# Batch 0's head: x loaded ahead of the weights, group 0's tile from scores of tokens and shifted tokens, groups 1 to 3 from the regular stage B, other idle products

## The chip, the core and the metric

The kernel runs on one NeuronCore of a Trainium2 chip. TensorE (PE) multiplies and transposes into PSUM, VectorE (DVE), ScalarE (ACT) and GpSimd (POOL) do the elementwise work, SyncE (SP) issues nearly all DMA transfers, in order, on one queue. The metric is device microseconds of one execution, the median of the runs.

## The reference

Two layers follow each other on x of shape (4, 12608, 128). The first is attention through 32 learned inducing points; the second is a channel mix with a token shift. `w_k`, `w_v` and `w_r` come as float64, the rest as float32.

```python
h = mab(I, x)            # 32 inducing rows attend to 12608 tokens of a batch
a = mab(x, h)            # every token attends to the 32 rows of h
a_prev = shift(a, 1)     # the token before, zeros ahead of the first
xk = mu_k * a + (1 - mu_k) * a_prev
xr = mu_r * a + (1 - mu_r) * a_prev
v = relu(xk @ w_k) ** 2 @ w_v        # 128 -> 1024 -> 128
out = sigmoid(xr @ w_r) * v
# mab(q, kv): a = softmax(q @ kv.T / sqrt(128)), with 1e-9 added to the sum; a @ kv
```

Since `a = A @ h` with A of 32 columns, the kernel never forms `a`. It folds h into the weights (`W`, from `h * mu_k` and `h * (1 - mu_k)` times `w_k`; `Wg` likewise with `w_r`) and multiplies the attention weights A of a token and of the token before it by them.

## The kernel before

The four batches are worked on one after the other. A batch has 6 full blocks of 2048 tokens and a tail of 320 tokens. A full block is 4 groups of 512 tokens.

**Stage A** of a batch computes h: transpose x (`xt`), scores against the inducing rows, a running maximum, exponentials, and the sums `acc` and `sum`. For batch 0 it runs ahead of everything else, as the **head** (`stage_a_head`, called from `head`, L908 to L943): the blocks come in the order tail, 0 to 5, and for each block the order is maximum, exponentials, the product of the block before, transposes of the block after next, transposes of the exponentials, scores of the next block. For batches 1 to 3 it is spread over the units of the batch before (`stage_a`).

**Loads in the head.** SP's queue takes x in half blocks of 512 KB (L192, L211) and between them the weights (L95) in pieces of 512 KB, raw 64-bit words: two of `w_k`, two of `w_v`, one of 128 KB of `w_r`. Each weight piece is turned into float32 by six steps on VectorE, ScalarE and GpSimd (`exponent`, `mantissa`, `clamp`, `sign`, `low`, `power`, L103 to L133), and `w_v` is then split into a high and a low part (`wvh`, `wvl`, L160). These steps wait in the list `work`; `place(n)` emits the next n of them, and the table `PARTS` says how many at which point of which block.

**Combine** (`combine`) turns `acc` and `sum` into `hT` and `h4`; `wpart` then makes `W` and `Wg`. `spin` (L889) issues products whose results nobody reads, between the last transposes and the last block's product.

**Stage B** makes the tile R of a group: the scores of its tokens against h, a softmax over 32 rows, and the weights A split into a high and a low part, two slices of 512 columns. R has 128 rows: rows 0 to 31 the tokens, 32 to 63 the shifted tokens, 64 to 127 the same again. The regular `stage_b` handles a block of four groups: a 32 x 32 transpose on VectorE, maximum, subtraction, exponential, sum, reciprocal, product, transpose back, high and low part (`hl`); then `spread(i)` fills R of group i with three DMA transfers (one first column from the group before, rows 0 to 31, rows 32 to 63), and `double` copies rows 0 to 63 to 64 to 127 with one. All of them go through SP's queue.

Block 0 of batch 0 has its own code, `stage_b_head` (L684), called twice, for groups 0 and 1 and for groups 2 and 3. It turns the weights with TensorE and copies 32 rows at a time: for group 0 eight copies fill all 128 rows (L744 and L745, ScalarE and VectorE in turn), for groups 1 to 3 one copy each for the tokens and for the shifted tokens (L738, L739), the first column by DMA from the group before, and `double`.

**The unit loop** (L999) is the bulk of the time. A unit is a quarter of the hidden columns of one group: 4 units a group, 25 groups and 100 units a batch, 400 in all. Unit n does: six products of `up` (L782, for two units at every even n) into PSUM, `square` (relu on VectorE, L792; its square twice on ScalarE, L797 and L798; the low part on GpSimd, L800; at the units in `high_vector` the square that is rounded is VectorE's, L794), and six products of `down` (L811) of the unit four before. At units that are 1 modulo 4 `zgate` computes the sigmoid (L770, L772).

Everything else is hung on the units by `at(n, f)`: f is emitted at the end of unit n. Block j + 1's stage B starts at unit t + 12j + 1 of its batch and stage A of the next batch's block j at t + 12j, where t is

```python
t = b * UB + (1 if b == 0 else 0)     # L978, UB = 100 units
```

Stage B's exponential comes 3 units after its start, stage A's exponential 15 after its own. Both use another ScalarE table than the sigmoid; a change of table is an instruction of its own, ACT_TABLE_LOAD. There are 5 buffers for R. Each engine executes its instructions in the order in which they are emitted; the order is written out by hand.

## Time and profile before

| | |
|---|---|
| time, median of 3 runs | 1158.64 us (1156.19 to 1158.97) |
| profiled execution | 1160.58 us |
| its span | 1158.8 us |
| PE, DVE, ACT, POOL busy | 94%, 79%, 84%, 82% |
| head, to stage B's first transpose (L703) | 51.5 us |
| unit 0 begins (first L792) | 63.2 us |
| unit 4, unit 8 begin | 83.7, 103.5 us |
| batch 1's unit 0 begins | 368.6 us |
| last unit begins | 1148.2 us |

In the profile's rows stand the start in us, the duration in us, the engine, the line, the operation and `out<-in` with the shapes; what stands in brackets is the idle time of the engine ahead of it and what ended it. PEld is TensorE's loading of weights, SPq the issuing of transfers by SP. A row of a `windows` view has the window, its length, busy time and count for each engine, and at its end the granted TensorE clock (1.00 is full), the DMA engines' share and GB/s. The rows themselves stand in the prediction.

### The profile page before, as it was taken

To read this page: it belongs to the slowest core of one execution; us is meant where nothing else is said; L and a number is where in the kernel's file an instruction comes from. 1 tells how busy PE (TensorE), PEld (TensorE's weight loads), DVE (VectorE), ACT (ScalarE), POOL (GpSimd) and SP (SyncE) were. 2 spreads that over 40 slices of the span, in tenths; PEclk is the share of its full clock that TensorE was granted. 3 is DMA by queue.
4 is the path that set the end of the run, shared out by engine and by line. 5 is a ranking of instruction groups with operands and counts; after the bars stand their busy time and mean duration, and the time that the engine had idled before them with its cause. 6 is when DMAs were issued, how large, how long until landed. Compare 5 with 4: busy or idle time off the path is not lost.

```text
span 1158.8 us, 19210 instructions
## 1 busy us (share of the span) xinstructions
PE 1089.2 (94%) x6548; PEld 740.6 (64%) x6548; DVE 919.0 (79%) x1293; ACT 976.2 (84%) x1112; POOL 945.2 (82%) x413
## 2 busy tenths in 40 slices
PE   6768889889999989999999989999999999999997
PEld 4435556556667656666667656666666666677775
DVE  5666778788777979999777979999877878888665
ACT  5446879889999868989889878889898989999995
POOL 1135778768998878899988878899988999999996
PEclk9869999989999989999999989999999999999999
DMA  9212565655515566666534565676423345444422
GB/s 276 62 39 75 115 137 124 150 136 106 123 27 101 120 140 133 151 152 146 120 56 82 113 144 126 144 165 142 101 49 60 75 91 110 82 79 86 83 39 33
DMA packets 267601, 124.38 MB, mean 107 GB/s; under 512 B 225552, under 2 KB 246704, under 8 KB 265200
## 3 DMA queue, kind: packets, MB, share of 16 engines
q1 hardware_dynamic: 267168, 123.14, 49.7%
q8 instruction: 52, 0.85, 0.3%
q14 instruction: 45, 0.37, 0.1%
q10 hardware_dynamic: 336, 0.02, 0.0%
HBM read 28.07 MB, written 25.82 MB: 47 GB/s over the span
## 4 chain that ended last, share of the span: by engine, by line
PE 74%; DVE 9%; ACT 4%; DMA 4%; SPq 3%; POOL 3%; issue 2%; DVEq 0%; ACTq 0%; POOLq 0%
PE ps_v L811 41%; PE ps_a L782 23%; DVE k_t L792 4%; PE ps_v L770 3%; POOL kl L800 3%; PE pb_b L603 2%; DMA R<-R 2%; PE pb_a L361 1%; PE pb_a L430 1%; SPq L834 1%; ACT k_t L798 1%; DVE kh L794 1%; DMA xb<-in_x_dram 1%; SPq L95 1%; DMA kl<-in_x_dram 1%
## 5 line engine op out<-in xcount | busy, mean ns | idle before, releaser
L800 POOL TENSOR_TENSOR kl<-k_t,kh 128x1024 fp32r<-128x1024 f32 (+2 forms) x400 | 936.3, 2370 | 174.0 <-ACT k_t L798 136.2
L792 DVE TENSOR_SCALAR k_t<-ps_a 128x1024 f32<-128x1024 f32 (+1 forms) x400 | 477.9, 1198 | 115.7 <-PE ps_a L782 85.4
L798 ACT ACTIVATE k_t<-k_t 128x1024 f32<-128x1024 f32 (+1 forms) x400 | 418.1, 1047 | 65.2 <-DVE kh L794 30.0
L797 ACT ACTIVATE kh<-k_t 128x1024 fp32r<-128x1024 f32 (+1 forms) x352 | 365.0, 1037 | 69.7 <-DVE k_t L792 69.1
L782 PE MATMUL ps_a<-R,W 64*128 64x512 f32 (+1 forms) x2400 | 344.7, 414 | 37.6 <-DVE k_t L792 13.2
L782 PEld LDWEIGHTS ps_a<-R,W 64*128 64x128 f32 x2400 | 212.0, 187 | 167.9 <-issue 51.5
L811 PE MATMUL ps_v<-kh,wvh 128*128 128x512 f32 (+1 forms) x800 | 273.9, 424 | 1.0 <-ACT rT L772 0.9
L811 PE MATMUL ps_v<-kl,wvh 128*128 128x512 f32 (+1 forms) x800 | 249.3, 393 | 2.5 <-POOL kl L800 1.2
L811 PE MATMUL ps_v<-kh,wvl 128*128 128x512 f32 (+1 forms) x800 | 248.7, 392 | 0.0
L811 PEld LDWEIGHTS ps_v<-kh,wvh 128*128 128x128 f32 x800 | 133.3, 190 | 98.9 <-issue 42.5
L811 PEld LDWEIGHTS ps_v<-kl,wvh 128*128 128x128 f32 x800 | 150.8, 190 | 37.1 <-POOL kl L800 4.0
L811 PEld LDWEIGHTS ps_v<-kh,wvl 128*128 128x128 f32 x800 | 151.0, 190 | 33.7
L816 DVE TENSOR_TENSOR oT<-ps_v,rT 128x512 f32<-128x512 f32 (+1 forms) x100 | 67.1, 671 | 17.1 <-PE ps_v L811 16.3
L827 DVE STREAM_TRANSPOSE ot<-oT 128x512 f32<-128x512 f32 x96 | 67.1, 699 | 0.0
L770 PE MATMUL ps_v<-R,Wg 128*128 128x512 f32 (+1 forms) x198 | 61.2, 390 | 0.0
L794 DVE SCALAR_TENSOR_TENSOR kh<-ps_a,k_t 128x1024 fp32r<-128x1024 f32 x48 | 58.8, 1225 | 2.4
L772 ACT ACTIVATE rT<-ps_v 128x512 f32<-128x512 f32 (+1 forms) x99 | 57.3, 579 | 0.4
L333 DVE STREAM_TRANSPOSE xs<-xb 128x512 f32<-128x512 f32 x72 | 49.9, 694 | 7.0 <-DMA xb<-in_x_dram 6.6
L772 ACT ACT_TABLE_LOAD x35 | 44.9, 1283 | 0.6
L770 PEld LDWEIGHTS ps_v<-R,Wg 128*128 128x128 f32 x198 | 37.3, 189 | 9.1 <-DVE k_t L792 0.8
L603 PE MATMUL pb_b<-xt,hT 128*32 128x512 f32 x184 | 25.9, 637 | 3.6 <-DVE aT L703 3.6
L364 DVE TENSOR_REDUCE mx<-pb_a 128x1 f32<-128x512 f32 x18 | 12.5, 692 | 16.7 <-PE pb_a L361 16.7
(201 smaller groups left out, 543.8 us busy)
## 6 DMA issues: line engine op xcount, KB each, us to landing
R<-R SPq DMA_DIRECT2D x95, 256.0 KB, 3.1
out_dram<-ot SPq DMA_DIRECT2D x184, 128.0 KB, 3.3
xb<-in_x_dram SPq DMA_DIRECT2D x18, 1024.0 KB, 5.9
xt<-xs SPq DMA_DIRECT2D x288, 64.0 KB, 2.0
R<-hl SPq DMA_DIRECT2D x92, 128.0 KB, 2.3
R<-hl SPq DMA_DIRECT2D x92, 127.8 KB, 2.4
kh<-in_x_dram SPq DMA_DIRECT2D x4, 512.0 KB, 8.0
kl<-in_x_dram SPq DMA_DIRECT2D x4, 512.0 KB, 7.5
```

The costliest lines, as they stand in the source:

```text
L333: nc.vector.transpose(out=xs.rearrange("p (s q) -> p s q", q=M), in_=S.xb[j][:, :, M * c:M * (c + 1)])
L770: nc.tensor.matmul(out=ps[:, :w], lhsT=S.Wg, rhs=R[:, s, :w], start=(s == 0), stop=(s == 1))
L772: nc.scalar.activation(out=self.rT, in_=ps[:, :w], func=AF.Sigmoid)
L782: nc.tensor.matmul(out=ps[:, r, :w], lhsT=S.W[a][rows, u * P:(u + 1) * P], rhs=R[rows, k, :w], start=(n == 0), stop=(n == 2))
L792: nc.vector.tensor_scalar(out=k, in0=ps, scalar1=0.0, scalar2=None, op0=ALU.max)
L794: nc.vector.scalar_tensor_tensor(out=kh, in0=ps, scalar=0.0, in1=k, op0=ALU.max, op1=ALU.mult)
L797: nc.scalar.activation(out=kh, in_=k, func=AF.Square)
L798: nc.scalar.activation(out=k, in_=k, func=AF.Square)
L800: return lambda eng, a, z: eng.tensor_tensor(out=kl[:, :, a:z], in0=k[:, :, a:z], in1=kh.bitcast(F32)[:, :, a:z], op=ALU.subtract)
L811: nc.tensor.matmul(out=self.v, lhsT=wt[:, fc, :], rhs=kk[:, c, :], start=(fc == 0 and n == 0), stop=(fc == FC - 1 and n == 2))
L816: nc.vector.tensor_tensor(out=self.oT, in0=self.v, in1=self.rT, op=ALU.mult)
L827: nc.vector.transpose(out=ot[:, o:o + w], in_=self.oT)
```

## The change

The edits are these.

- **Loads.** All x of batch 0 is queued ahead of the five weight pieces, and `w_r` ahead of `w_v`. The conversion steps move to later blocks (`PARTS`): none before block 3, the conversions of `w_v` after the last block's maximum, the split of `w_v` after stage B's first steps.
- **Last block of the head.** The sum and `weights` come ahead of the transposes of the exponentials, and `weights` is cut in two (`weights`, `weights_sum`).
- **Idle products.** `spin` issues six transposes of 128 columns where there were fourteen products of 512.
- **Group 0.** `stage_b_first` takes the scores of group 0's tokens and of the same tokens shifted by one. The shifted ones are in `S.x0`, a copy that GpSimd makes early in the head in one of R's buffers. Weights of tokens and shifted tokens are laid out so that four transposes give all 128 rows of R for the high part and four for the low one; two copies fill R.
- **Groups 1 to 3** come from the regular `stage_b(0, 0)`, whose steps are called by hand: the scores to the subtraction among the steps of `stage_b_first`, the exponential in unit 0, the rest at the end of unit 0. Then `spread` and `double` run through SP's queue.
- **Unit numbers.** In batch 0 t is 4 where it was 1, so that the stages on the blocks come three units later (block 1's stage B at unit 2, one unit later). In later batches the combine's steps come one unit and block 0's stage B three units sooner.

Group 0 needs no transfer for R before or after; groups 1 to 3 needed two each and now need four. SP's queue from the load of batch 1's first block on, before (`R<-R` with 32x2x1 is the first column, `R<-R` with 64x1024 `double`, `xt<-xs` stage A):

```order
L206 DMA xb<-in_x_dram 128x2048
L336 DMA xt<-xs 32x512 x4
L570 DMA R<-R 32x2x1
L336 DMA xt<-xs 32x512 x4
L577 DMA R<-R 64x1024
L336 DMA xt<-xs 32x512 x8
L570 DMA R<-R 32x2x1
L577 DMA R<-R 64x1024
```

and with the change:

```order
L206 DMA xb<-in_x_dram 128x2048
L580 DMA R<-hl 32x2x1
L593 DMA R<-hl 32x1024
L593 DMA R<-hl 32x2x511
L587 DMA R<-R 64x1024
```

These four of group 1 are followed by the same four of group 2 and three of group 3, then by the first four `xt<-xs` and group 3's `double`.

ScalarE at a block's two exponentials in batch 0 (`e1t` is stage A's, `s` stage B's, `rT` the sigmoid), before:

```order
L397 ACT_TABLE_LOAD
L397 ACTIVATE alpha<-mkr,nb 128x1
L398 ACTIVATE e1t,ss<-pb_a,nb 128x512
L798 ACTIVATE k_t<-k_t 128x1024
L772 ACT_TABLE_LOAD
L772 ACTIVATE rT<-ps_v 128x512
L620 ACT_TABLE_LOAD
L620 ACTIVATE s_1652<-s_1652 128x512
```

and with the change:

```order
L401 ACT_TABLE_LOAD
L401 ACTIVATE alpha<-mkr,nb 128x1
L402 ACTIVATE e1t,ss<-pb_a,nb 128x512
L806 ACTIVATE k_t<-k_t 128x1024
L630 ACTIVATE s_1687<-s_1687 128x512
L805 ACTIVATE kh<-k_t 128x1024
L806 ACTIVATE k_t<-k_t 128x1024
L780 ACT_TABLE_LOAD
L780 ACTIVATE rT<-ps_v 128x512
```

The sigmoid has moved behind both exponentials, so that one table load between them is gone and the sigmoid's own one follows them. ScalarE has 26 table loads up to the 25th sigmoid before and 18 with the change.

VectorE from the copy of the last block's exponentials (`e`) to `hT`, before:

```order
L274 COPY e_654<-pb_a 128x512
L279 SCALAR_TENSOR_TENSOR sum<-sum,alpha,ss 128x1
L500 TENSOR_TENSOR ws<-sum,wt 128x1
L504 TENSOR_SCALAR rd<-pb_b 128x1
L505 RECIPROCAL rd<-rd 128x1
L508 TENSOR_SCALAR mk<-stack,wt,rd 128x32
L297 SCALAR_TENSOR_TENSOR acc<-acc,alpha,pb_a 128x128
L518 COPY hT<-pb_b 128x32
```

and with the change:

```order
L278 COPY e_643<-pb_a 128x512
L127 SCALAR_TENSOR_TENSOR s_593<-s_593,aT 128x512
L105 TENSOR_SCALAR s_647<-k_t 128x512
L514 TENSOR_SCALAR rd<-pb_b 128x1
L515 RECIPROCAL rd<-rd 128x1
L518 TENSOR_SCALAR mk<-stack,wt,rd 128x32
L115 TENSOR_SCALAR xs<-k_t 128x512
L109 TENSOR_SCALAR s_647<-s_647 128x512
L301 SCALAR_TENSOR_TENSOR acc<-acc,alpha,pb_a 128x128
L120 TENSOR_SCALAR aT<-k_t 128x512
L528 COPY hT<-pb_b 128x32
```

Five conversion steps of `w_v` have come in between. The last two of the second piece (L123, L127) stand behind `h4`, ahead of stage B's first transpose (L714); the first piece's other five stand ahead of these rows, behind the last block's maximum.

The diff, cut to its core:

```diff
+                if j == 0 and h + i == 0:
+                    S.x0 = r_pool.tile([P, 2, G], F32, name="R")[:, 0, :]
+                    nc.gpsimd.memset(S.x0[:, 0:1], 0.0)
+                    nc.gpsimd.tensor_copy(out=S.x0[:, 1:], in_=dst[:, :G - 1])
...
     def weights():
         ws = S.sum
         if ahead:
-            wt = sm.tile([P, 1], F32, name="wt")
+            wt = L["wt"] = sm.tile([P, 1], F32, name="wt")
             nc.scalar.activation(out=wt, in_=S.mrun, func=AF.Exp, bias=L["nm"], scale=scale)
             ws = sm.tile([P, 1], F32, name="ws")
             nc.vector.tensor_tensor(out=ws, in0=S.sum, in1=wt, op=ALU.mult)
+        L["ws"] = ws
...
         return prod, high, low
     if ahead:
-        return maxes, weights, hfin, wpart
-    at(t + 9, weights)
-    at(t + 10, hfin)
+        return maxes, weights, weights_sum, hfin, wpart
+    at(t + 8, weights)
+    at(t + 9, hfin)
     for gate in range(2):
         prod, high, low = wpart(gate, lambda: pb_tile("a"))
-        at(t + 11 + 2 * gate, prod)
-        at(t + 11 + 2 * gate, high)
-        at(t + 12 + 2 * gate, low)
+        at(t + 10 + 2 * gate, prod)
+        at(t + 10 + 2 * gate, high)
+        at(t + 11 + 2 * gate, low)
...
+    if at is None:
+        return scores, trans, maxi, sub, expo, total, recip, mult, back, high, low, spread
...
+def stage_b_first():
     S = batches[0]
+    n = 2 * Q
     L = {}
     def scores():
+        ps = L["ps"] = pb_tile("a")
+        pv4 = ps[:, :n * M].rearrange("(i m) (c w p) -> i m w c p", m=M, w=2, p=M)
+        for w, src in enumerate((S.xt[0, 0], S.x0)):
+            xv = src.rearrange("c (k i p) -> c i k p", i=Q, p=M)
             for i in range(Q):
+                nc.tensor.matmul(out=pv4[i, :, w], lhsT=S.hT, rhs=xv[:, i], start=True, stop=True)
     def diff():
+        s2 = L["s2"] = st.tile([P, Q, P], F32, name="e1").rearrange("p k (i m) -> p (k i) m", m=M)[:, :n, :]
         nc.vector.transpose(out=s2.rearrange("p k m -> p (k m)"), in_=L["ps"][:, :n * M])
         mx = sm.tile([P, Q * Q], F32, name="mx2")[:, :n]
         nc.vector.tensor_reduce(out=mx, in_=s2, op=ALU.max, axis=AX.X)
...
         nc.vector.tensor_scalar(out=sm2, in0=sm2, scalar1=EPS, scalar2=None, op0=ALU.add)
         nc.vector.reciprocal(out=sm2, in_=sm2)
         nc.vector.tensor_tensor(out=s2, in0=s2, in1=sm2.unsqueeze(2).broadcast_to([P, n, M]), op=ALU.mult)
+        nc.vector.memset(s2[0:1, 1, :], 0.0)
+    def src():
+        return L["s2"].rearrange("p (c w) m -> p c (w m)", w=2).unsqueeze(2).broadcast_to([P, Q, 2, 2 * M])
+    def half(s):
+        return L["a"][:, s, :].rearrange("p (c r k) -> p c r k", c=Q, r=2)
     def high():
+        L["a"] = st.tile([P, 2, G], F32R, name="hl", bufs=2)
+        nc.scalar.copy(out=half(0), in_=src())
     def low():
+        nc.vector.tensor_tensor(out=half(1), in0=src(), in1=half(0).bitcast(F32), op=ALU.subtract)
+    def turn(s):
+        if s == 0:
+            L["pt"] = pa.tile([P, 2, G], F32, name="ps_a")
+            S.R[0] = r_pool.tile([P, 2, G], F32R, name="R")
+        for c in range(Q):
+            cs = slice(c * P, (c + 1) * P)
+            nc.tensor.transpose(out=L["pt"][:, s, cs], identity=ident, in_=L["a"].bitcast(F32)[:, s, cs])
+    def put(s):
+        if s == 0:
+            nc.scalar.copy(out=S.R[0][:, 0, :], in_=L["pt"][:, 0, :])
+        else:
+            nc.vector.tensor_copy(out=S.R[0][:, 1, :], in_=L["pt"][:, 1, :])
+    return scores, diff, expo, norm, high, low, turn, put
 NG = (NBLK - 1) * Q + 1
-    def put(k, whole):
-        g = gs[k]
-        ps = pa.tile([P, 2, G], F32, name="ps_a")
-        for s in range(2):
-            for c in range(Q):
-                nc.tensor.transpose(out=ps[:M, s, c * P:(c + 1) * P], identity=ident,
-                                    in_=L["a"].bitcast(F32)[:, k * Q + c, s, :])
-        new_r(S, g)
-        R = S.R[g]
-        if not whole:
-            nc.scalar.copy(out=R[:M], in_=ps[:M])
-            nc.vector.tensor_copy(out=R[M:HP, :, 1:], in_=ps[:M, :, :G - 1])
-            return
-        nc.vector.memset(R.bitcast(F32)[3 * M:, :, 0:1], 0.0)
-        for s in range(2):
-            for r in range(2):
-                nc.scalar.copy(out=R[HP * r:HP * r + M, s], in_=ps[:M, s])
-                nc.vector.tensor_copy(out=R[HP * r + M:HP * (r + 1), s, 1:], in_=ps[:M, s, :G - 1])
-    return scores, diff, expo, norm, high, low, put
...
+wloads += [load_wr]
-wloads += [load_wr]
-    if wloads:
-        wloads.pop(0)()
-maxes, weights, hfin, wpart = combine(0)
+maxes, weights, weights_sum, hfin, wpart = combine(0)
...
-    half = P // 2
-    rhs = wvh.rearrange("p c d -> p (c d)")[:, :G]
-    for i in range(3):
-        nc.tensor.matmul(out=ps[:, i % 2, :], lhsT=wvh[:, i, :], rhs=rhs, start=True, stop=True)
-        for r in range(2):
-            rows = slice(half * r, half * (r + 1))
-            nc.tensor.matmul(out=ps[:, r, :], lhsT=wvh[rows, (i + r) % FC, :], rhs=rhs[rows],
-                             start=True, stop=True)
-    for i in range(3):
-        nc.tensor.matmul(out=ps[:, i % 2, :], lhsT=wvh[:, i, :], rhs=rhs, start=True, stop=True)
-PARTS_FIRST = 6
-PARTS = ((0, 0, 0), (3, 3, 0), (3, 3, 0), (3, 3, 0), (3, 3, 1), (1, 0, 0), (0, 0, 0))
+        nc.tensor.transpose(out=ps[:, 0, :P], in_=ident, identity=ident)
+PARTS = ((0, 0, 0), (0, 0, 0), (0, 0, 0), (0, 3, 0), (3, 3, 0), (3, 3, 1), (3, 4, 2))
...
         if k + 2 < NBLK:
             ab[k + 2].tr()
         place(PARTS[k][1])
+        if k == last:
+            ab[k].sums()
+            weights()
         ab[k].etrans()
         ab[k].ecopy()
-        ab[k].sums()
         if k < last:
+            ab[k].sums()
             ab[k + 1].scores()
         place(PARTS[k][2])
-    spin(4)
-    weights()
+    weights_sum()
+    place(2)
+    spin(6)
     ab[last].hmm()
     ab[last].acc()
     load_x(1, 0)
+    place(1)
     hfin()
-    assert not work
+    place(2)
 events = {}
...
-    sc0, df0, ex0, nm0, hi0, lo0, put0 = stage_b_head([0, 1])
-    sc1, df1, ex1, nm1, hi1, lo1, put1 = stage_b_head([2, 3])
+    scores, diff, expo, norm, high, low, turn, put = stage_b_first()
+    (b_scores, b_trans, b_maxi, b_sub, b_expo, b_total, b_recip, b_mult, b_back, b_high, b_low,
+     b_spread) = stage_b(0, 0, None, 0)
-    run([sc0, df0, wk[0], ex0, wk[1], nm0, wk[2], hi0, lo0, lambda: put0(0, True)])
-    at(0, lambda: put0(1, False))
-    for n, f in ((0, sc1), (1, lambda: double(batches[0], 1)), (1, df1), (1, ex1), (2, nm1), (2, hi1),
-                 (2, wg[0]), (2, wg[1]), (3, wg[2]), (3, lo1)):
+    run([scores, b_scores, diff, wk[0], expo, b_trans, norm, wk[1], high, wk[2], lambda: turn(0),
+         lambda: put(0), low, lambda: turn(1), b_maxi, lambda: put(1), b_sub])
+    soon(0, b_expo)
+    for n, f in ((0, b_total), (0, b_recip), (0, b_mult), (0, b_back), (0, b_high), (0, b_low),
+                 (0, wg[0]), (1, wg[1]), (1, wg[2]), (3, lambda: units[0][0].zgate())):
-    for k in range(2):
-        at(4 + 2 * k, lambda k=k: put1(k, False))
-        at(5 + 2 * k, lambda k=k: double(batches[0], 2 + k))
-    at(4, lambda: units[0][0].zgate(first=True))
+    for i in range(1, Q):
+        at(i - 1, lambda i=i: b_spread(i))
+        at(i, lambda i=i: double(batches[0], i))
+    place(len(work))
-    t = b * UB + (1 if b == 0 else 0)
+    t = b * UB + (4 if b == 0 else 0)
-        stage_b(b, j + 1, at, s + 1 if b or j else 1)
+        stage_b(b, j + 1, at, s + 1 if b or j else 2)
-        stage_b(b + 1, 0, at, s + 13)
+        stage_b(b + 1, 0, at, s + 10)
```

More of the change, by code (lines that the diff above doesn't have):

```diff
@@ L500, in weights, with weights_sum @@
                 nc.vector.tensor_tensor(out=ws, in0=S.sum, in1=wt, op=ALU.mult)
+            L["ws"] = ws
+            if not ahead:
+                weights_sum()
+        def weights_sum():
+            ws, wt = L["ws"], L.get("wt")
             ps = pb_tile(None if ahead else "b")
@@ L514, in hfin @@
         def hfin():
-            ps = pb_tile(None if ahead else "b")
+            ps = pb_tile("b")
             nc.tensor.matmul(out=ps[:, :M], lhsT=S.acc, rhs=L["sw"], start=True, stop=True)
@@ L717, in norm @@
             nc.vector.tensor_tensor(out=s2, in0=s2, in1=sm2.unsqueeze(2).broadcast_to([P, n, M]), op=ALU.mult)
+            nc.vector.memset(s2[0:1, 1, :], 0.0)
[3 more added lines that the diff above has]
+            return L["a"][:, s, :].rearrange("p (c r k) -> p c r k", c=Q, r=2)
         def high():
-            a = L["a"] = st.tile([P, 2, G], F32R, name="hl", bufs=2) \
-                .rearrange("p s t -> p (s t)")[:, :2 * n * M].rearrange("p (k s m) -> p k s m", s=2, m=M)
@@ L759, in __init__, with zgate @@
             self.v = None
-        def zgate(self, first=False):
+        def zgate(self):
             S, w = self.S, self.w
             R = S.R[self.g]
-            if first:
-                ps = pb_tile("a")
-            else:
-                ps = self.v = pv.tile([P, G], F32, name="ps_v")[:, :w]
+            ps = self.v = pv.tile([P, G], F32, name="ps_v")[:, :w]
             for s in range(2):
@@ L913, in head @@
             ab[k].tr()
-        place(PARTS_FIRST)
         ab[0].scores()
```

17 lines of the change are left out of this document (3 added, 14 removed).

## The prediction, written before the changed kernel was timed

> **What bounds the kernel now.** I read the page first, then the rate of the unit loop (one unit is one `k_t` row: 256 of the 1024 hidden columns of one 512-token group), then the stretches where it is slow, and last the head.
>
> ```profile
> span 1158.8 us, 19210 instructions
> PE 74%; DVE 9%; ACT 4%; DMA 4%; SPq 3%; POOL 3%; issue 2%; DVEq 0%; ACTq 0%; POOLq 0%
> ```
>
> Over the whole span the end is set by TensorE, which the change leaves alone nearly everywhere. The 26% of the chain that is not PE is where it can act. To place it I count units per stretch, VectorE's `k_t` instruction (L792) in chosen windows:
>
> ```profile
> 63.20:83.60 20.40, 4.89 (x4) 0.75 0.23 52
> 83.60:103.50 19.90, 4.89 (x4) 0.80 0.22 47
> 103.50:307.00 203.50, 81.66 (x68) 0.97 0.57 127
> 368.50:378.50 10.00, 4.83 (x4) 1.00 0.67 135
> 399.00:414.40 15.40, 4.83 (x4) 0.93 0.66 135
> 378.50:566.00 187.50, 82.40 (x68) 0.98 0.64 144
> 646.50:833.30 186.80, 82.39 (x68) 0.98 0.61 136
> ```
>
> Columns: window, length, busy (count), granted clock, DMA share, GB/s. Units 0 to 7 take 40.3 us; four units at the same place of batch 1 take 10.0. Units 8 to 75 take 203.5 us in batch 0, and the 68 units 96 later take 187.5 in batch 1 and 186.8 in batch 2. So batch 0 loses some 20 us in its first eight units and 16 more in the next 68, beside the 63 us ahead of unit 0.
>
> **The 16 us: what batch 0 does differently.** ScalarE's rows around the two exponentials of a block, first in batch 0, then in batch 1:
>
> ```profile
> 173.18 1.28 ACT L772 ACT_TABLE_LOAD   x1
> 174.48 0.60 ACT L772 ACTIVATE rT<-ps_v 128x512 f32<-128x512 f32 x1
> 175.09 1.28 ACT L620 ACT_TABLE_LOAD   x1
> ...
> 453.16 0.61 ACT L620 ACTIVATE s<-s 128x512 f32<-128x512 f32 x1
> ```
>
> In batch 0 a sigmoid falls between the exponential of stage A (L398) and that of stage B (L620), so each table is loaded once more. In batch 1 the two follow each other. Batch 0's blocks start at unit 1 + 12j, those of later batches at a multiple of 4, and the sigmoid comes at every unit that is 1 modulo 4. The change starts batch 0's blocks at 4 + 12j: a multiple of 4, and ScalarE's instructions stand in batch 0 as in batch 1 (the second order fence ahead).
>
> ```profile
> 103.50:307.00 203.50, 171.55 (x187) 0.97 0.57 127
> 378.50:566.00 187.50, 161.69 (x179) 0.98 0.64 144
> ```
>
> ScalarE's windows: 187 instructions and 171.6 us against 179 and 161.7. The 8 instructions are table loads, 8 x 1.28 = 10.2 us; the rest of the 16 is what waits behind them. I take the whole 16.0 (203.5 less 187.5), since work and order are then those of batch 1. One thing stays worse: block 1's first tile (unit 16) is spread at unit 12 and doubled at 14, in batch 1 at the 11th and 13th after its start, and there the four units ahead of it take 15.4 us where others take 10. One unit later is 2.6 us (187.5 / 68) at most, nothing at least, if the shorter queue ahead of it makes it up. I take 1.4. **Term: -14.6.**
>
> **The head.**
>
> ```profile
> 8.81 3.74 PE L229 MATMUL ps_a<-ident,kh 128*128 128x128 f32 x16 [4.56 <-DMA kh<-in_x_dram]
> 15.60 1.27 POOL L133 TENSOR_TENSOR wk_sb<-e1t,s 128x512 f32<-128x512 f32 x1 [14.30 <-DVE s L127]
> 25.68 1.06 PE L229 MATMUL ps_a<-ident,kl 128*128 128x128 f32 x8 [0.66 <-DMA kl<-in_x_dram]
> 29.40 0.43 DVE L105 TENSOR_SCALAR s<-k_t 128x512 int32<-128x512 int32 x1
> 31.07 0.69 DVE L123 SCALAR_TENSOR_TENSOR e1t<-k_t,e1t 128x512 f32<-128x512 uint32 x1
> 34.65 0.23 DVE L105 TENSOR_SCALAR s<-oT 128x128 int32<-128x128 int32 x1
> 38.47 0.15 DVE L250 TENSOR_SCALAR nb<-mx 128x1 f32<-128x1 f32 x1
> 42.48 0.15 DVE L250 TENSOR_SCALAR nb<-mx 128x1 f32<-128x1 f32 x1
> 44.76 0.69 DVE L274 COPY e<-pb_a 128x512 f32<-128x512 f32 x1 [0.81 <-PE pb_a L269]
> 46.48 0.97 PE L902 MATMUL ps_a<-wvh 128*128 128x512 f32 x3
> 47.50 1.08 PE L286 MATMUL pb_a<-xb,e 128*32 128x128 f32 x32
> 51.46 0.45 DVE L703 STREAM_TRANSPOSE s<-pb_b 128x256 f32<-128x256 f32 x1 [1.15 <-PE pb_b L697]
> ```
>
> Two half blocks' worth of 512 KB have landed at 8.81, twelve at 25.68: 1.69 us each. Ahead of 25.68 those twelve are four blocks and four weight pieces; now they are all of batch 0's x, and the first weight lands at 27.4, the next at 29.1, w_r at 29.5, w_v at 31.2 and 32.9. So blocks no longer wait for data, but the first conversion (L105) stands on VectorE behind block 3's maximum and waits there until 27.4; behind it in the queue is the copy of block 3's exponentials. Its three operations and that copy end at 29.3, block 4's maximum at 30.6. A block with a full conversion takes 5.2 us (L105 at 29.40, then 34.65), one without 4.0 (L250 at 38.47, then 42.48). With 5.0 and 4.5 for the two that are left the last block's maximum is done at 40.1, for 42.48 before.
>
> From there to stage B's first transpose it was 9.0 us (42.48 to 51.46). The idle products go: they end at 47.45, and the copy of exponentials that the block product at 47.50 needs is done at 45.45, so -2.0. But both w_v conversions now stand there on VectorE, four operations of 0.43 (L105) and two of 0.69 us (L123) each, 6.2 us, 6.7 with the end of w_r's, of which I put 3.1 in gaps where it waited: 9.0 - 2.0 + 3.6 = 10.6, and the transpose at 50.7. The bounds: all of the 6.7 on the path 53.8, all in gaps 47.1; the middle, because half of the rows stand behind a wait for ScalarE. The copy for shifted tokens is one GpSimd instruction of 128 x 511; a product of that size took 1.27 us there (L133), and the engine had been idle for 14.3 us ahead of it: nothing, and 1.3 if a conversion had to wait for it.
>
> **The first tile.**
>
> ```profile
> 54.27 0.42 DVE L717 TENSOR_TENSOR s<-s,sm 128x256 f32<-128x256 f32 x1
> 55.18 1.89 PE L733 MATMUL ps_a<-ident,hl 128*32 128x128 f32 x8 [2.14 <-ACT hl L722]
> 57.11 0.57 ACT L744 CAST R<-ps_a 32x512 fp32r<-32x512 f32 x1 [1.98 <-PE ps_a L733]
> 63.24 1.22 DVE L792 TENSOR_SCALAR k_t<-ps_a 128x1024 f32<-128x1024 f32 x1 [0.88 <-PE ps_a L782]
> ```
>
> From the transpose (51.46) to unit 0 it was 11.8 us, 5.3 of them the eight copies of 32 rows that ScalarE and VectorE make in turn (57.11 to 62.4). Now the tile is turned as 128 rows. To the division 3.2 as before, regular stage B's transpose in a gap 0.5, the high half 0.6 behind the weights' cast 0.4, low 0.7, four transposes 0.95, the second copy 0.7, stage B's subtraction 0.7, gaps 0.55: 8.3, and unit 0 at 59.0. **Term: -4.2** (-8 to -1 with the head's bounds).
>
> **Units 0 to 8.**
>
> ```profile
> 67.57 1.21 DVE L739 CAST R<-ps_a 32x1022 fp32r<-32x1022 f32 x1 [2.48 <-ACT R L738]
> 82.31 1.65 PE ps_a L782 x6
> 83.96 2.86 PE ps_v L811 x6
> 112.26 1.21 SPq L583 DMA_DIRECT2D R<-hl  x2
> R<-R SPq DMA_DIRECT2D x95, 256.0 KB, 3.1
> R<-hl SPq DMA_DIRECT2D x92, 127.8 KB, 2.4
> ```
>
> Groups 1 to 3 lose three times a copy on ScalarE and one of 1.21 us on VectorE (L739), 24 transposes of the kind that took 1.89 for 8, and the second small softmax. In their place each group has four transfers where it had two, in SP's queue ahead of nearly all x transposes (the first order fence ahead). Group 1: after unit 0's `k_t` (1.2) VectorE runs sum, reciprocal, product, transpose back and low half with ScalarE's high half between, 0.7 + 0.2 + 0.3 + 0.7 + 0.7 + 0.6 + 0.7 and 0.1 of gaps, to 64.2. Three issues of 0.6, landing 2.4, doubling 3.1: 71.5. Its first six products 1.65 at half clock (a row of the chain of waits, as the next): unit 4 at 73.2, for 83.66. SP waits at each doubling for the transfers ahead, so group 2 is there 4.7 us later, before unit 8 needs it. Units 4 to 7 take 10.0 as in batch 1, and 3.0 for what half a clock does to some and the start's own table loads: unit 8 at 86.2, for 103.5. Bounds: the 3.0 could be 0 or 7 and the transfers 2 us either way. **Term, beside the head's -4.2: -13.1.**
>
> From batch 1 on the combine comes one unit and the next batch's block 0 three units earlier. The four units at a batch's start take 10.0 us, so there is no stall to win: 0. If TensorE now has to wait for VectorE's `hT` (one unit lies between, where there were three), it is a microsecond at each of three boundaries, inside the bounds below.
>
> **Sum:** -4.2 - 13.1 - 14.6 = -31.9. The profiled span of 1158.8 becomes 1126.9, its execution's 1160.58 becomes 1128.7; the median of the runs shown, 1158.64, lies 1.9 below that execution, so I forecast **1127 us** as the median.
>
> **The clock.** The granted clock, in windows of all engines:
>
> ```profile
> 44.00:50.00 6.00, 4.89 (x54) 3.53 (x54) 2.45 (x11) 0.03 (x1) 0.00 (x0) 1.00 0.38 156
> 50.00:66.00 16.00, 10.91 (x52) 5.21 (x52) 8.45 (x20) 5.06 (x9) 0.00 (x0) 0.52 0.01 1
> ```
>
> With the idle products in, it was 1.00 to 50 and 0.52 in the next 16 us. Six transposes are in their place, so the drop may come some 5 us sooner. TensorE has little on the path there: the block product, whose 1.08 us would double, and two small ones, about 1.5 us in all, which the head's bounds hold. The Trainium skill ("TensorE: Matmul & The Clock Gate", Part 4) says that a transpose does not count as activity for the clock gate the way a product does, which speaks against this swap. By that rule the early drop is certain and the sum is 1128 rather than 1127. The trace neither shows nor excludes it: the head's transposes at a granted 1.00 stand among ordinary products.
>
> **Rivals.**
>
> ```profile
> 222.53 8.67 DMA xb<-in_x_dram
> ```
>
> (A) Batch 0 keeps its rate after unit 8: then not the table loads held it, but its transfers. For it speaks this wait of 8.67 us for an x block in batch 0's chain; against it, that batches 1 and 2, with the same transfers, agree to 0.7 us. Price 14.6: **1141.** Chance 0.16. (B) Group 1's transfers come so late through SP's queue that unit 4 starts no sooner than at 83.7, 10.5 later than forecast: **1137.** For it: four waits stand in a row on one queue; against: no store stands in it yet. 0.12. (C) Slower: without the 512-column products TensorE's clock, once halved, stays so far into the unit loop. A unit's six up and six down products took 1.65 + 2.86 = 4.5 us at the half clock, so half of it, 2.25 us, is lost in each unit in which TensorE sets the pace. Beyond those counted, 14 such units eat the 32 us; at 24, unit 32, it is 1127 + 54 = **1181.** For it: 0.52 from 50 to 66 and 0.75 to 0.80 up to unit 8; against: 0.97 over the 68 units after that. 0.08, of which 0.03 ends near no change. The forecast has 0.64, and 1117 to 1138 as its own range (head -2 to +3, tile and transfers -3 to +3, units 4 to 7 -3 to +4, the rest -2 to +1).
>
> About 0.3% is what a measurement of this kernel can tell from no change. Forecast, A and B are all beyond it: faster 0.92, same 0.03, slower 0.05. The range 1116 to 1143 takes in A and B.
>
> **What would show it.** Right: unit 0 near 59 and unit 4 near 73; eight table loads fewer; 68 units from unit 8 in some 189 us. Wrong: VectorE held at L105 well past 27.4; unit 4 waiting for `R<-R`; a clock near 0.5 beyond 90 us; units 8 to 75 still at 203.

## The result: 1140.8 us, and the profile after

The changed kernel takes 1140.80 us (median of 4 runs, 1139.67 to 1141.39), the kernel before in the same comparison 1157.41 (4 runs, 1151.20 to 1158.97). The ratio is 0.9865, with a 95% interval of 0.9827 to 0.9904: faster by 1.35%. The forecast was 1127 within 1116 to 1143. The direction and the range held, but the time lies 13.8 us above the forecast and 2.8 us outside the 1117 to 1138 that the likeliest case had as its own. About half of the 32 us is missing. The time is the 1141 that the prediction gave for rival A, but A's mechanism did not come (experiment 1); the two agree by chance.

The profiled execution took 1141.06 us. From its page, the span and the chain of waits by engine:

```profile
span 1139.2 us, 19132 instructions
PE 76%; POOL 5%; DVE 5%; issue 4%; SPq 4%; DMA 3%; ACT 2%; DVEq 0%; ACTq 0%; POOLq 0%
```

ScalarE's share of the chain has halved (4% to 2%) and VectorE's fell from 9% to 5%; GpSimd's and SP's shares have risen. VectorE's `k_t` (now L800) and ScalarE in windows, for the same units as in the prediction: units 0 to 3, 4 to 7, 8 to 75, then units 30 and 31, and ScalarE over units 8 to 75 (window, length, busy time and count, granted clock, DMA share, GB/s):

```profile
64.40:77.70 13.30, 4.80 (x4) 0.70 0.29 60
77.70:92.20 14.50, 4.78 (x4) 0.76 0.51 113
92.20:286.20 194.00, 82.36 (x68) 0.97 0.61 137
156.40:166.40 10.00, 2.44 (x2) 0.91 0.75 148
...
92.20:286.20 194.00, 160.14 (x177) 0.97 0.61 137
```

By the prediction's terms, to 0.1 us: unit 0 begins 1.2 us later than before (64.46 for 63.24), where 4.2 earlier was forecast. Units 0 to 7 take 27.8 us for 40.3, a gain of 12.5 where 13.1 was forecast. Units 8 to 75 take 194.0 for 203.5, a gain of 9.5 where 14.6 was forecast. From unit 76 to the last unit it is 842.3 for 841.1, a loss of 1.2 where nothing was forecast. The sum is 1.2 - 12.5 - 9.5 + 1.2 = -19.6, which is what the two spans differ by (1158.8 and 1139.2). Two terms are wrong, by 5.4 and 5.1 us, and one by 1.2.

**The head**, on VectorE (start, duration, and in brackets the idle time ahead and what ended it):

```profile
29.82 0.43 DVE L105 TENSOR_SCALAR s<-k_t 128x512 int32<-128x512 int32 x1 [4.38 <-DMA k_t<-in_moe_w_k_dram]
32.48 0.15 DVE L254 TENSOR_SCALAR nb<-mx 128x1 f32<-128x1 f32 x1
35.55 0.43 DVE L105 TENSOR_SCALAR s<-k_t 128x512 int32<-128x512 int32 x1 [1.13 <-POOL wk_sb L133]
41.55 0.23 DVE L105 TENSOR_SCALAR s<-oT 128x128 int32<-128x128 int32 x1 [1.13 <-POOL wk_sb L133]
43.74 0.15 DVE L254 TENSOR_SCALAR nb<-mx 128x1 f32<-128x1 f32 x1
44.86 0.43 DVE L105 TENSOR_SCALAR s<-k_t 128x512 int32<-128x512 int32 x1 [0.57 <-POOL wr_sb L133]
51.04 0.43 DVE L105 TENSOR_SCALAR s<-k_t 128x512 int32<-128x512 int32 x1 [1.38 <-POOL ot L133]
55.44 0.44 DVE L714 STREAM_TRANSPOSE e<-pb_a 128x256 f32<-128x256 f32 x1
64.46 1.23 DVE L800 TENSOR_SCALAR k_t<-ps_a 128x1024 f32<-128x1024 f32 x1 [0.30 <-PE ps_a L790]
```

The first weight is there at 29.82, where I had 27.4. Each later conversion waits for GpSimd's last product of the one before (`power`, L133), since there is one buffer each for two of its operands: 1.13 + 1.13 + 0.57 + 1.38 = 4.2 us of waits that the prediction does not have.

**Group 8's tile.** Around unit 30, SP's queue and the piece of the chain that holds unit 32 up:

```profile
157.93 3.01 SPq L842 DMA_DIRECT2D out_dram<-ot  x4
160.99 0.80 SPq L587 DMA_DIRECT2D R<-R  x1
...
160.99 3.73 DMA R<-R
```

The transfer that completes R of group 8 (needed from unit 32) stands behind the four stores of groups 4 and 5 and lands at 164.72. Units 30 and 31 take 10.0 us where two units take 5.5 (187.5 / 68 x 2).

### The profile page after: what moved, and what is told of

Its sections match the earlier page's. It is cut to its first block, busy times and chain, and to the rows that moved or that the text cites. A ratio compares the mean times of both kernels' runs of the same rounds, so it can differ in the third digit from the quotient of the medians.

```text
span 1139.2 us, 19132 instructions
## 1 busy us (share of the span) xinstructions
PE 1080.6 (95%) x6508; PEld 742.2 (65%) x6508; DVE 910.4 (80%) x1287; ACT 962.0 (84%) x1098; POOL 945.9 (83%) x415
## 4 chain that ended last, share of the span: by engine, by line
PE 76%; POOL 5%; DVE 5%; issue 4%; SPq 4%; DMA 3%; ACT 2%; DVEq 0%; ACTq 0%; POOLq 0%
PE ps_v L819 43%; PE ps_a L790 23%; POOL kl L808 5%; PE ps_v L778 4%; PE pb_b L613 2%; DVE k_t L800 2%; DMA R<-R 2%; PE pb_a L365 2%; PE pb_a L434 2%; SPq L192 1%; SPq L842 1%; ACT k_t L806 1%; SPq L211 1%; SPq L340 1%; DMA R<-hl 1%
## 5 line engine op out<-in xcount | busy, mean ns | idle before, releaser
L800 DVE TENSOR_SCALAR k_t<-ps_a 128x1024 f32<-128x1024 f32 (+1 forms) x400 | 478.4, 1200 | 121.9 <-PE ps_a L790 91.1
L790 PE MATMUL ps_a<-R,W 64*128 64x512 f32 (+1 forms) x2400 | 339.2, 412 | 25.2 <-DMA R<-R 20.2
L778 PE MATMUL ps_v<-R,Wg 128*128 128x512 f32 (+1 forms) x200 | 63.8, 401 | 0.1
L133 POOL TENSOR_TENSOR wk_sb<-e1t,s 128x512 f32<-128x512 f32 x2 | 2.5, 1270 | 29.5 <-DVE s L127 29.5
```

Source lines behind the costliest of these rows:

```text
L778: nc.tensor.matmul(out=ps[:, :w], lhsT=S.Wg, rhs=R[:, s, :w], start=(s == 0), stop=(s == 1))
L790: nc.tensor.matmul(out=ps[:, r, :w], lhsT=S.W[a][rows, u * P:(u + 1) * P], rhs=R[rows, k, :w], start=(n == 0), stop=(n == 2))
L800: nc.vector.tensor_scalar(out=k, in0=ps, scalar1=0.0, scalar2=None, op0=ALU.max)
```

## The experiments

Times are medians. The kernel before stood beside each set: 1158.86 us (10 runs, 1156.34 to 1162.32) for the first four, 1156.26 (13 runs, 1153.05 to 1159.62) for the next four, 1159.34 (7 runs, 1154.73 to 1160.37) for the last two. Ratios are to these. The changed kernel was not run again beside them. Differences to it are taken between the times themselves, whose runs agree to 2.6 us or better (but for the second and the seventh experiment's, which spread over 8 us); a difference of 1.5 us is the least that I read, and one near it is weak unless the profile shows where it comes from. By the ratios, whose denominator, the kernel before, spreads over 5.6 to 7.8 us, the differences come out up to 3.4 us otherwise (experiment 3: 4.7 instead of 1.7; experiment 4: 13.8 instead of 10.4; experiment 2: 11.2 instead of 13.8); no sign changes.

**1. The place of the blocks alone.** The kernel before, with batch 0's blocks at 4 + 12j, and what has to move at the end of batch 0:

```diff
-        t = b * UB + (1 if b == 0 else 0)
+        t = b * UB + (4 if b == 0 else 0)
...
-            combine(b + 1, at, s)
-            stage_b(b + 1, 0, at, s + 13)
+            combine(b + 1, at, s - (1 if b == 0 else 0))
+            stage_b(b + 1, 0, at, s + (10 if b == 0 else 13))
```

> The kernel before, with batch 0's blocks starting at unit 4 + 12j instead of 1 + 12j (and the combine one unit, block 0 of batch 1 three units sooner after it); head, group 0's tile and loads as before. Theory (place of the blocks): units 8 to 75 go from 203.5 us to about 194, as in the changed kernel: 16 less for the pace of batch 1, 6 to 7 lost at unit 32, whose R is now doubled 3 units ahead of its need. The total falls by about 9, to 1148. Rival (the start): the pace of units 8 to 75 came from the new start and the emptier queue behind it; then the 203.5 us stay and the total is within 3 us of before.

Measured: 1143.02 (1142.32 to 1144.35), ratio 0.9858 (0.9837 to 0.9880), 15.8 us faster than before, where 9 were expected. The loss at units 30 to 34 came as expected (16.9 us for 12.6 before and 10.1 in batch 1). But units 8 to 30 took 6.5 us less than the same units of batch 1, and units 0 to 7, for which nothing was expected, 35.8 us for 40.3.

**2. All of the change but the place.** The changed kernel with `t = b * UB + (1 if b == 0 else 0)`:

```diff
-        t = b * UB + (4 if b == 0 else 0)
+        t = b * UB + (1 if b == 0 else 0)
```

> The changed kernel with batch 0's blocks back at unit 1 + 12j; all else as changed. Theory (place of the blocks): units 8 to 75 take about 203 us again instead of 194, the wait for R at unit 32 goes, the total rises by 8 to 10, to about 1150. Rival (the start): 194 us stay, total about 1141.

Measured: 1154.59 (7 runs, 1150.61 to 1158.39), ratio 0.9962 (0.9938 to 0.9986): 13.8 us slower than the changed kernel (8 to 10 were expected), 4.3 faster than before. The profiled execution, 1151.64, is one of its faster ones. ScalarE over units 8 to 75, first in experiment 1 and then in experiment 2:

```profile
99.70:288.10 188.40, 157.98 (x175) 0.98 0.63 142
...
91.80:298.00 206.20, 173.49 (x188) 0.97 0.55 121
```

The place alone brings batch 0 close to batch 1's pace (188.4, batch 1 had 187.5) and its absence takes it back (206.2; 203.5 before). Between the two ScalarE has 13 instructions and 15.5 us more for the same work; 11 of the 13 are table loads (21 for 10; 20 before, 11 in the changed kernel), 14.1 us. So rival A (batch 0 keeps its rate whatever the order) falls. The chain of waits says the same. Before, it runs through all three table loads of a block at three blocks, here the first (start, duration, engine, line):

```profile
169.96 1.28 ACT L397
173.18 1.28 ACT L772
175.09 1.28 ACT L620
```

That is 9 x 1.28 = 11.5 us of the chain over units 8 to 75, and the same nine stand in experiment 2's. In the chains of experiment 1 and of the changed kernel there is no table load in these units. The wait of 8.67 us for x, to which rival A pointed, is gone from the chains of all three, although experiment 2 is slow. What is left open is whether anything else that moves with the place has a part in the 17.8 us between 188.4 and 206.2; no run moved the sigmoid alone. The rest of the change gains 11.6 us by unit 8 in experiment 2's profile (91.87 for 103.50) and gives 2.7 of it back up to unit 76.

**3. Two buffers for a conversion.** The changed kernel, with two of the conversion's operands in a tile of two buffers:

```diff
-                X.t = st.tile([P, G], I32, name="s2")[:, :n]
+                X.h = st.tile([P, 2, G], F32, name="hl", bufs=2)
+                X.t = X.h.bitcast(I32)[:, 0, :n]
...
-                X.q = st.tile([P, G], F32, name="e1t", bufs=1)[:, :n]
+                X.q = X.h[:, 1, :n]
```

> The changed kernel with two sets of work buffers for the conversion of the weights, so that the first step of a piece does not wait for GpSimd's last step of the piece before. Theory (the conversions stand on VectorE's path in the head): the four waits of L105 for GpSimd's product, 1.13 + 1.13 + 0.57 + 1.38 = 4.2 us, go, unit 0 begins 3 to 4 us sooner, total about 1137.5. Rival (the head is held by the late landing of the weights and by ScalarE's steps): the waits only move to the next step, unit 0 less than 1 us sooner, total about 1140.5.

Measured: 1139.11 (1138.92 to 1139.52), ratio 0.9824 (0.9803 to 0.9844), 1.7 us below the changed kernel: between the theory and the rival. VectorE's first step (now L106) and GpSimd's product (L134):

```profile
34.06 1.46 DVE L106 TENSOR_SCALAR hl<-k_t 128x512 int32<-128x512 int32 x1
39.87 1.26 DVE L106 TENSOR_SCALAR hl<-oT 128x128 int32<-128x128 int32 x1
43.56 0.42 DVE L106 TENSOR_SCALAR hl<-k_t 128x512 int32<-128x512 int32 x1
...
33.97 1.27 POOL L134 TENSOR_TENSOR wk_sb<-hl 128x512 f32<-128x512 f32 x1 [24.43 <-DVE hl L128]
39.77 1.28 POOL L134 TENSOR_TENSOR wk_sb<-hl 128x512 f32<-128x512 f32 x1 [4.53 <-DVE hl L128]
```

The wait for the buffer is gone, but where this step begins while GpSimd's product runs, it ends only after it: 1.46 us instead of 0.42, and 1.26 for the small one, which takes 0.23 in the changed kernel. So where two of the waits were, nearly the same time is spent inside the instruction. The Trainium skill ("SBUF — State Buffer", the section on SBUF's two separate sides) says that GpSimd and some of VectorE's instructions (those in a mode that uses two ports, or with two inputs in SBUF) share a pair of ports as an exclusive lock, and that the later one blocks wholly. These rows agree: both end 0.1 to 0.3 us after the product. Of the gain 0.65 us stand at the last block's maximum (43.09 for 43.74), 0.28 of them because the first weight came that much sooner (29.54); the rest comes behind it, where the waits of 0.57 and 1.38 us were.

**4. Group 8's tile four units earlier.** The changed kernel with block 2's stage B at unit 13 instead of 17:

```diff
-            stage_b(b, j + 1, at, s + 1 if b or j else 2)
+            stage_b(b, j + 1, at, (2, 13)[j] if b == 0 and j < 2 else s + 1)
```

> The changed kernel with block 2's stage B in batch 0 at unit 13 instead of 17, so that group 8's R is doubled 7 units ahead of its need, as in batch 1. Two more table loads on ScalarE, 2.6 us. Theory (R of group 8 is late): the loss of 7.2 us between units 30 and 34 goes, total lower by 4 to 7, about 1136. Rival (that wait is only what shows of a queue that is full anyway): the transfers wait elsewhere and the total stays within 2 us of 1141.

Measured: 1130.40 (1129.09 to 1130.95), ratio 0.9746 (0.9725 to 0.9768), 10.4 us below the changed kernel. SP's queue at the doubling of group 8 in this kernel, the stores that stood ahead of it in the changed kernel, and units 8 to 75 and 30 to 31 in windows:

```profile
140.93 0.50 SPq L587 DMA_DIRECT2D R<-R  x1
155.39 3.01 SPq L842 DMA_DIRECT2D out_dram<-ot  x4
...
91.20:277.10 185.90, 82.27 (x68) 0.99 0.64 143
155.00:160.40 5.40, 2.44 (x2) 1.00 0.81 134
```

The doubling is issued 14 us before the stores and 20 us sooner than in the changed kernel, the stall is gone (5.4 us for two units), and units 8 to 75 take 185.9. In the spans (1139.2 and 1128.2) that is 8.2 of 11.0; 0.9 more lies ahead of unit 8, where the first weight came 1.0 us sooner in this execution, and 1.8 behind unit 75. So the lateness is worth some 8 us in its own stretch, more than the 4 to 7 expected. Where the 1.8 comes from was not looked into; experiments 9 and 10, with the same edit, have it too (839.8 and 840.8 from unit 76 to the last for 842.3). The two more table loads are there (13 for 11 in units 8 to 75) and stand nowhere in the chain.

**5. w_k ahead of the last two blocks of x.** In the changed kernel's loop over the loads:

```diff
         load_x(0, j, pairs if j < 4 else None)
+        if j == 3:
+            wloads.pop(0)()
+            wloads.pop(0)()
```

> The changed kernel with w_k's two halves loaded ahead of the last two blocks of x instead of behind them (the order of the other transfers stays). In the changed kernel's trace VectorE waits at the first conversion (L105) 4.4 us for the first weight, until 29.82, and I count this wait as the first part of the 5.4 us by which unit 0 missed its forecast. Theory: with the weight there at about 25 the wait goes, and the next blocks stand 3 us earlier; something under 4.4 remains, because block 4's scores on TensorE end at 28.2 and its maximum stood at 31.6: 1137.5 us beside 1140.8, unit 0 at 61 instead of 64.5. Rival: the last blocks' x now comes 3.4 us later and takes the wait over, or the conversions that follow are held by GpSimd's products anyway: 1140.5.

Measured: 1137.04 (1135.99 to 1138.26), ratio 0.9833 (0.9807 to 0.9859), 3.8 us below the changed kernel. Unit 0 begins at 60.84, where 61 was expected. VectorE there:

```profile
23.87 0.42 DVE L105 TENSOR_SCALAR s<-k_t 128x512 int32<-128x512 int32 x1
27.13 0.69 DVE L278 COPY e<-pb_b 128x512 f32<-128x512 f32 x1 [2.17 <-PE pb_b L273]
29.07 0.15 DVE L254 TENSOR_SCALAR nb<-mx 128x1 f32<-128x1 f32 x1
```

The first conversion no longer waits, block 4's maximum is done at 29.22 instead of 32.63, and unit 0 begins 3.6 us sooner; in the spans 2.8 of it are left at the end (1136.4 for 1139.2), in the medians 3.8. Part of the wait has turned into one for TensorE (2.17).

**6. Full idle products in TensorE's gaps.** The changed kernel, with ten products where they fit between 43 and 60 us in place of the six transposes (two inside `maxes`, one behind it, one behind the last transposes of exponentials, two in place of `spin(6)`, four behind the product for `W`):

```diff
-    def spin(n):
+    def warm(n):
         ps = pa.tile([P, 2, G], F32, name="ps_a")
         for i in range(n):
-            nc.tensor.transpose(out=ps[:, 0, :P], in_=ident, identity=ident)
+            nc.tensor.matmul(out=ps[:, i % 2, :], lhsT=ident, rhs=wk_sb[:, :G], start=True, stop=True)
```

> The changed kernel with ten full idle products (128 rows by 512 columns, float32, of w_k) in the gaps of TensorE between 43 and 60 us, in place of the six transposes: two and one around the combine's small products, one behind the last transposes of exponentials, two where the six transposes stood, four behind the product for W. Their results are not used. In the changed kernel the granted clock is 0.76 at 44 to 46, 0.50 at 46 to 52 and 0.50 again at 60 to 64. Theory: full products hold the clock where the transposes did not: 1.00 up to 56 at least, the last block's product 1.1 us instead of 1.73, and 1 to 2 us less in the whole: 1139.3 beside 1140.8. Rival 1: the clock falls between 44 and 50 all the same (the gaps are due to it by time, not by the kind of work) and the products only stand in the way: 1141 to 1144. Rival 2: the clock holds, but VectorE sets the pace there and nothing is won: 1140.8.

Measured: 1140.20 (1139.58 to 1140.74), ratio 0.9859 (0.9835 to 0.9884): the same as the changed kernel within the runs. All engines in three windows, first in the changed kernel, then here (PE, PEld, DVE, ACT, POOL, the granted clock):

```profile
42.00:50.00 8.00, 4.11 (x52) 3.22 (x53) 6.43 (x21) 2.81 (x8) 0.71 (x2) 0.69 0.38 133
50.00:58.00 8.00, 5.17 (x69) 2.61 (x67) 6.66 (x20) 1.91 (x4) 2.28 (x2) 0.88 0.00 0
58.00:66.00 8.00, 5.46 (x30) 3.29 (x30) 5.71 (x12) 3.29 (x7) 2.54 (x2) 0.57 0.00 0
```

```profile
42.00:50.00 8.00, 7.47 (x59) 3.58 (x59) 5.68 (x19) 2.29 (x6) 1.26 (x2) 1.00 0.38 133
50.00:58.00 8.00, 6.47 (x73) 3.03 (x73) 7.14 (x22) 2.04 (x4) 1.73 (x2) 1.00 0.00 0
58.00:66.00 8.00, 5.82 (x38) 2.76 (x36) 6.84 (x14) 4.88 (x7) 2.54 (x2) 1.00 0.01 2
```

The clock is held at 1.00 for 24 us, and the whole is the same. The profiles say where. From the last block's maximum to the first tile's transpose it is 11.9 us, 11.7 in the changed kernel: there rival 2 holds, VectorE sets the pace. From that transpose to unit 0 it is 7.8 us for 9.0 (8.6 to 9.1 in the other kernels with this tile and without the full products): there TensorE counts, and the products are worth about 1 us, as the theory had it. It does not show in the total, because from unit 76 on this kernel takes 1.8 us longer (844.1 for 842.3); the kernels with the same order there (the changed one and experiments 3, 5, 6 and 8) lie between 841.9 and 844.1, and why was not looked into.

**7. The idle products alone.** The kernel before with the changed kernel's `spin(6)` of transposes.

```diff
-        spin(4)
+        spin(6)
```

> The kernel before with six idle transposes in place of its fourteen idle products: this part of the change alone. The prediction's sum takes 2.0 us for it (the products end at 47.45, the copy that the block product needs is done at 45.45): ratio 0.998, 1156.9 beside 1158.9, with the last block's product starting near 46. Rival: the clock drops earlier without the products, as in the changed kernel (0.50 from 46), and what is won is lost in the block product and the transposes of the first tile: 1158.4 to 1160.

Measured: 1158.13 (10 runs, 1154.44 to 1162.88 but for one of 4886.93), ratio 1.0019 (1.0001 to 1.0037): nothing is won, at most something lost. TensorE in this kernel, and VectorE's sum behind the product:

```profile
44.77 0.82 PE L893 MATMUL ps_a<-ident 128*128 128x128 f32 x6
46.20 0.56 PE L502 MATMUL pb_b<-ws,stack 128*128 128x1 f32 x2 [0.61 <-DVE ws L500]
46.69 1.93 PE L286 MATMUL pb_a<-xb,e 128*32 128x128 f32 x32
...
48.69 0.35 DVE L297 SCALAR_TENSOR_TENSOR acc<-acc,alpha,pb_a 128x128 f32<-128x128 f32 x1 [1.20 <-PE pb_a L286]
```

The block product begins 0.81 us sooner (47.50 before) and not 2.0, because the sum's two products (L502) and the wait for them stand ahead of it. It takes 1.93 us instead of 1.08, at a granted clock of 0.50 instead of 1.00: it ends 0.04 later. Stage B's first transpose comes 0.4 us later (51.87 for 51.46).

**8. No idle work.** The changed kernel without `spin(6)`.

```diff
         place(2)
-        spin(6)
         ab[last].hmm()
```

> The changed kernel without its six idle transposes. In its trace they take 1.52 us on TensorE at 49.03, behind them stands the last block's product (50.48), whose result VectorE adds at 52.65, some 0.9 us after the last operand of the combine (mk, 51.77) is made. Theory: the transposes neither hold the clock (0.50 with them) nor cost more than those 0.9 us: between 1140.0 and 1140.8, the same. Rival: they do keep the clock from a longer fall, and without them units 0 to 8 are 1 to 3 us slower: 1142 to 1144.

Measured: 1138.94 (1137.61 to 1140.17), ratio 0.9851 (0.9820 to 0.9882). That is 1.9 us below the changed kernel, more than the 0.8 expected and not the rival's loss. But in its profile the first weight also came 1.45 us sooner (the first L105 at 28.37), with nothing changed ahead of it, and 1.7 of the 2.0 us by which unit 0 is earlier stand already at the last block's maximum (42.03 for 43.74). What the transposes cost is at most some tenths of a us; it isn't settled.

**9. Three edits together.** Those of experiments 3, 4 and 5 (where the expectation says block 1's tile, it is block 2's, as in experiment 4).

> The changed kernel with three edits at once: block 1's tile made at its fixed early place in batch 0, two buffers for the conversion, and w_k ahead of the last two blocks of x. If they save in different places, their gains add: 10.4 + 1.7 + 3.8 from 1140.8 gives 1125. If two buffers save the same time as the earlier weight (both shorten VectorE's row of conversions ahead of the last block's maximum), 1.7 less is gained: 1126.5. If the early tile depends on what the queue of transfers has done at that moment, it is not there and the result lies at 1135.

Measured: 1125.58 (1124.66 to 1125.96), ratio 0.9723 (0.9695 to 0.9750): the gains add (15.9 were expected of the sum). The version beats both kernels, the changed one by 15.2 us. Units 0 to 7 and 8 to 75:

```profile
59.60:86.70 27.10, 9.57 (x8) 0.80 0.41 90
86.70:272.40 185.70, 82.27 (x68) 0.99 0.63 143
```

**10. The same and the full idle products.**

> The same three edits with the ten full idle products in TensorE's gaps from 43 to 60 us, which kept the granted clock at 1.00 up to 66 us and made the whole 0.6 us shorter by themselves. With the conversions shorter, less stands on VectorE in that stretch, so TensorE's small products and the first units should count for more: 1 to 2 us below the kernel with three edits. Rival: the products take the place of idle time that is no longer there, and it is 0 to 1 us slower.

Measured: 1125.75 (1125.26 to 1126.20), ratio 0.9723 (0.9700 to 0.9746): the same; the 1 to 2 us did not come. As in experiment 6 the way from the first tile's transpose to unit 0 is shorter (7.9 us for 8.6); 0.3 is lost ahead of it and 1.1 behind unit 76.

## Why the prediction was right and wrong

**The range and the sign were right, the time was 13.8 us off.** The range holds because it was drawn to take in the prices of rivals A and B; the forecast's own 1117 to 1138 does not hold, nor do the bounds of the head's term (-8 to -1, measured +1.2). The failed steps are two terms, the head's and that of units 8 to 75, whose gains were forecast too large by 5.4 and 5.1 us. Smaller parts are 0.6 at units 0 to 8, 1.2 at the boundaries, and 1.6 because the median lies 0.3 below the profiled execution, where I had put it 1.9 below.

**Units 0 to 8: right, step by step.** Rival B (late transfers) did not come. The order of the chain was: VectorE's softmax after unit 0, then SP. I had the first issue 5.2 us after unit 0 begins; it is 5.18. TensorE and SP in the changed kernel:

```profile
69.64 0.75 SPq L580 DMA_DIRECT2D R<-hl  x1
73.63 0.52 SPq L587 DMA_DIRECT2D R<-R  x1
76.61 1.65 PE L790 MATMUL ps_a<-R,W 64*128 64x512 f32 x11 [0.55 <-DMA R<-R]
80.84 1.22 PE L819 MATMUL ps_v<-kh,wvh 128*128 128x512 f32 x2 [2.59 <-ACT rT L780]
```

The first products of group 1 wait for `R<-R` as the forecast's sum has it (the list of signs, in contradiction to that sum, named this wait as one of being wrong), and unit 4 begins 13.3 us after unit 0, for 14.2. Units 4 to 7 took 14.5 for 13.0: the 3.0 that I had put there for half a clock and the start's table loads were 4.5 (2.59 of them this wait for the sigmoid, behind its table load). What the term leaves out is the place: in experiment 1 it alone takes 4.5 us off units 0 to 7, and without it (experiment 2) they take 28.7 us. So the new start brings 11.6 by itself, and most of the place's 4.5 is the same time.

**Units 8 to 75: mechanism right, one wait missed.** The eight table loads are gone (62 in the whole for 70), and those left in these units are off the chain. The step that failed is "since work and order are then those of batch 1", with its "One thing stays worse". Once past the start the pace is batch 1's: from unit 40 to 80 the distance between a unit and the one 96 later in the kernel before is constant within 0.2 us. But the four units by which batch 0's blocks start later than those of later batches make each tile four units later against its need, and I counted that for group 4 alone. Group 4's lateness, which I took as 1.4 (half of one unit, which is 187.5 / 68 = 2.8 us and not the 2.6 that stands there), came out as -1.2: the units after the stall run faster and make it up by unit 30. Group 8's, which I did not look at, cost 7.7 from unit 30 to 40, 7.2 of it by unit 34, and was not made up. In the chain the issue of four stores (2.6 us) and the doubling itself (3.7 us) stand there; what the stores cost by themselves was not separated from the lateness. So 187.5 - 1.2 + 7.7 = 194.0, where I had 187.5 + 1.4. Experiment 4 makes block 2's tiles four units earlier, and units 8 to 75 take 185.9.

**The head: the step from "the first weight lands at 27.4" to "the last block's maximum is done at 40.1" failed.** It was 43.74. First, the landing of the first weight: 29.82 instead of 27.4; VectorE is held at L105 that long, a sign of being wrong that the prediction names. The 1.69 us for each 512 KB is a mean over two kinds of loads. In the trace of before a piece of x lands 1.7 to 1.8 us after the one ahead of it, a piece of the weights 1.3 to 1.6 us, and what stands ahead of the first weight now is x alone: the last of x lands at 27.1, where the sum has 25.7. (The last two blocks come in pieces of 256 KB, L211, not of 512.) The first weight follows 2.7 us later, and 1.3 to 2.4 us later in the executions of experiments 2, 3, 4, 6 and 8, so up to 1.4 us of this step differ from one execution to the next. Experiment 5 prices the wait at 2.8 us in the spans and 3.8 in the medians. Then, the steps between conversions: I took a block with a full conversion at 5.2 and one without at 4.0 us from rows in which the conversions lay further apart; here each waited for GpSimd's product of the one before. The way from the first L105 to the last block's maximum took 13.9 us for 12.7. Experiment 3 shows that a second buffer takes away only part of it (1.7 us on the whole), since VectorE's step is then held up by GpSimd's product inside the instruction.

**The idle products** I had at -2.0; experiment 7 shows 0. The step "they end at 47.45, and the copy of exponentials that the block product at 47.50 needs is done at 45.45, so -2.0" left out the sum's two products, which stand ahead too, and what the idle products did for the next one: it is 0.81 us sooner and 0.85 longer. With the sentence from the Trainium skill ("TensorE: Matmul & The Clock Gate", Part 4: a transpose does not count as activity the way a product does) the prediction made it 1128 for 1127, 1 us for an early drop of the clock. Experiment 7 agrees with the drop (0.50 during the block product, 1.00 before) and nearly with its price. But its six transposes are also less work (0.8 us on TensorE where the fourteen products took 3.1), so it does not show that the kind of work is the reason. The prediction's "about 1.5 us in all, which the head's bounds hold" had the size and stood in no term. In the changed kernel the low clock costs nothing up to the first tile's transpose, where VectorE sets the pace, and about 1 us from there to unit 0 (experiments 6 and 10). The transpose L714 comes 11.7 us after the last maximum, for 10.6 forecast, and unit 0 9.0 us after L714, for 8.3.

**Rival C** (the clock stays low far into the units) did not come: 0.70 and 0.76 in units 0 to 7, 0.97 over units 8 to 75, as before.

**Boundaries: 0 forecast, 1.2 lost** from unit 76 to the end, inside the bounds that I had set. Kernels with the same order there differ by 2.2 us (experiment 6), so the 1.2 can't be put down to anything; it was not looked into.

## What to carry to other kernels

When a stage is moved to where another batch has it, compare not only its place in the period but also the distance from each of its products to their first use, for every instance and with what stands ahead of them in the queue: here one tile cost half of what the move was to bring. Idle work that keeps a clock up is worth what it does for the work behind it, not the time that it occupies; here removing it left the whole time as it was, and so did holding the clock, since another engine set the pace in most of the stretch. And where conversions are pushed together, read from the rows which buffer and which second engine each of them waits for, since durations taken from places where they lay apart do not hold.

## What the runs showed of the hardware that was not expected

- A 128x512 integer operation of VectorE of 0.42 us took 1.46 us when it began during a product of GpSimd of the same size (experiment 3). For this operation a second buffer therefore did not overlap the two engines; two operations on 128x1 during another such product took 0.15 and 0.16 us, no more than elsewhere.
- Ten products of 512 columns between 43 and 59 us held the granted clock at 1.00 from 42 to 66 us, where six transposes and the kernel's own work had 0.69, 0.88 and 0.57 in the three thirds (experiment 6). The ten took 9.7 us of TensorE and the six 1.5, so this does not tell the kind of work from its amount.
- The first weight piece landed at 28.2 to 29.8 us in six kernels with the same loads (29.82, 28.18, 29.54, 28.81, 28.95 and 28.37 in the changed kernel and experiments 2, 3, 4, 6 and 8), though the last of x ahead of it landed at 26.9 to 27.1 in all. In the three of them that have the same head, unit 0 moved with it: 64.46, 63.16 and 63.52 in the changed kernel and experiments 2 and 4.
- The kernels with batch 0's blocks at 1 + 12j spread widely over their runs (the kernel before over 5.6 to 7.8 us in each set, experiment 2 over 7.8), those with the blocks at 4 + 12j by 2.6 us or less in four runs each. Why was not followed up.
